# Attention with rotary embedding, then an MLP: batch 0's queries rotated in two parts, tables loaded by ScalarE, squares summed by adds

## The chip, the core and the metric

The kernel runs on one core of a Trainium2 chip. The core has five engines that run side by side, each with its own queue in order: TensorE (PE; matrix products, with weight loads as PEld), VectorE (DVE), ScalarE (ACT), GpSimd (POOL) and SyncE (SP), which here issues DMA transfers. The metric is the device time of one execution in microseconds; lower is better.

## The reference

Attention over 4 batches of 8 heads, 576 positions of 64 columns, then an MLP over the 2304 rows of 512 that come out:

```python
q_rot, k_rot = rotate(q), rotate(k)          # x1*cos - x2*sin, x1*sin + x2*cos
scores = (q_rot @ k_rot.T) / 8
attn = exp(scores - max); attn = attn / (sum(attn) + 1e-9)
x = (attn @ v), heads side by side           # 2304 x 512
h = x @ w_in                                 # 512 x 2048
g = s * relu(h)**2 + b
out = g @ w_out                              # 2048 x 512
```

`w_in` and `w_out` arrive as float64 words and are turned into float32 on the chip.

## The kernel before

**Tiling.** Two heads make a pair, so there are 16 pairs, four to a batch. The 576 positions of a pair are 4 x 128 main rows and a tail of 64 for each head; a score tile is 128 queries by 576 keys, nine tiles to a pair (i = 0 to 8, the ninth holds both tails). The 2304 rows of x are cut into nine units: unit 0 and units 1 to 7 of 256 columns each (two to a batch), and unit 8 with the tails of all batches.

**Two precisions.** Batch 0 (pairs 0 to 3, `FQ`) works in float32: key and query are rotated (`rotate`, three VectorE or GpSimd steps: x times sine into z, x times cosine in place, x plus z), transposed on TensorE (`qk_T`) and copied out of PSUM (`qk_ev`); `s_pair` makes the scores of two tiles at once. The later pairs are split into a high and a low float16 half and transposed by DMA. Then, for every tile: `s_max` (VectorE, the row maximum), `s_exp` (ScalarE), the sum's reciprocal, and the scaled tile as float16 in two halves (`p_a`, `p_b`, the tile pab), which SP transposes by DMA into pt. For two tiles (i = 0 and 2) of each pair of batch 0 TensorE transposes instead. `pv_sum` multiplies pt by v, and `o_out` (ScalarE) writes the result into x.

**The weights.** 32 blocks of 512 KB are loaded, made into float32 (`w_sign`, `w_low`, `w_rebias`, `w_join`), measured (`w_gram` on TensorE, `w_max` on VectorE), and once all 16 of a matrix are there, split into float16 halves (`w_hi`, `w_lo`).

**The MLP.** Unit 0 runs in float32 early on (`mlp_in0`, `mlp_out0`). The other eight units need a power-of-two scale for x: `x_norm` (ScalarE) squares x into bfloat16, `x_sum` (TensorE, L828) sums the squares over the 512 columns of d by four products with a matrix of ones, one for each slot of 128, `x_scale` (VectorE, seven short steps, the first a maximum) makes the scale, `x_hi` and `x_lo` the float16 halves. Then 16 blocks of `mlp_in` (L863), the squared relu, its halves g, and `mlp_out` (L930).

**What sets the order.** `plan()` lists the work as pieces with the engines that may do each and the tokens that it reads and writes. ORDER is a permutation of these pieces, two characters for each; PICKS says which engine does a piece that several could do; SLOTS says which buffer of a kind a piece takes. The pieces are issued in that order, so each engine's queue is a part of it, and an engine whose next instruction waits does nothing else meanwhile. SP's queue holds all DMA issues. PSUM has two banks px for short results.

**The start.** SP issues the rope table (cosine, sine, minus sine, 432 KB), the identity, the first key, the first v, a weight block and the first two queries.

Of the kernel before, what the change touches and what calls it, by code (L numbers as in the profile page):

```python
# [20 lines left out]
GP = 4  # L21
P_SCALE = 2.0 ** 14
# [16 lines left out]
    "AADTEBADDUEAD_AJDcDdECEDEEDeDfEFDiDgELDhEMAEEIENAFAMDjALA3AKANAdDkDlJjAGA5EJAHAfA6AeDrDpAgDsJkAhEGA4JlA9DqEHEKA7DtJrJsJt"  # L39
    "DyA-DVAOAIEODuAPDvDwD1DxJuJmDWDXD2D3EPESEQBAAwAWDYJnDZAXA_DzBBJoEXEVAYJvAZD6AxAzD7ERAyD0A0AaEeAqArDaEYEZEfD4EWD5AtEaEhEb"  # L40
    "DbAQJ0BCJpA8D8ATEsAjAmASAsEcAuEgARJ8ETJ1AlAkJ9J2J-DmBRBEJ3JqAUJ_AnBDEiEdBTBFBUEjEvE5ErBGABD9BrEkAiBSAoAvBHA1A2BIE6KAJ4Bt"
    "BVEmElEnBxJwEoJxDnKFAVAbB0ByKNApKGBsBXEuJ5BzE2B1BYD-DoKHKOBZBaKIKJBbBuEpBKKPJ6J7BMFGBeFFFJBvK4BgKQBLK5AcBNBOE7JyK6KKBfLA"
    "KBBJBPJzKCLBB2BwBQK7FILCBhBkBWKLKWBcFTE3BiFULDB3BlEtBnBmEwKMKRB4KeKXKDLEB7B6CSLFKfKYBoB5E4KSKnFhB-BdK8FVKZKEB8KaKgKTFQCU"
    "CVKhKvKbKUClKiK9CTKcCWBjBpB_CBKoKwKdCABqCCKpCoKqKxKjK-B9CDLJCEKrLKCmEqKkCnCpLLKlCLCNKsKyLRcdLrCYACKmLMLNKVKzCOCbLSLTKtLs"
    "CMLULOLVbMbNbObLK_LGLtCabPLHLIbQLuCZCPCyFHCsC1C0EULWLPK0CcLacebRLiExEycfLvEzLjLkF7cgCtE0E1CuFKE-F-CzC2chLlLbbSbTCvCXCdCe"
    "ciLmE_CwMRMSLnLXLQLYE8C_CFDBLcDCLdLeLwLZMTMUDADDLfCHLgbWbXbYbVbZbaFkK1KuL3MVL4MECfDMF6bgK2bfL5MFE9LxFRCIChCiF9K3L0MCbiL1"
    "MWcjbhbjDNCgL2CGbUbkCJbbCxC3MXGHGICjMDDPL6MGFSL7ckC4LhLoLpLqL_MdCQCKb2b0L8DOMHMeMAFAMIC5DGFfLyMBLzCRMqC6MfMLL9L-MMMJCkCq"
    "M3bcb3M4CrMNMrMKFiC8M5C7M6clFLb1DHFMcmC9FNFOFPM7Fqb4b5M8MabdDEC-MbMoMcFYM9MgDQMhMpMlMsFWcncoMtMONANBNOFCMiMxMmDFFDMZFrDI"
    "MuMvFXMjMybeb6b7blDRb8cpMQNPNCDJMPDKNDNQNENRNFNGNSMnF5MwMkMYMzFEFZNHNTcqbmbnbsNmDLbpbqbrN0DSNnNIF8NXNUNJNLNoFgbtbucrGVFa"
    "FBM0FsGENVGFNYFcN1FjM1M2NdGGNeNMNfNgNhNicBFlcAb_Npb-NqFmN2FnNjNrNscCcDN3M_M-NKFdNZNNNWFtFuFvdDNtFoFecsboODbvdEbwb9cEN4Fp"  # L50
    "dFOEFwFyNxNuctN5GJFxNydGOFcuN9dHFzdINaOROGcFcJcGN6NccvF2NbN-OHcwOINvOSN7F_GAcIOUcLcKOJHJcxOKcyGTFbOVGBOTNzGUGYGXczOLGCGD"
    "OMNlF3NwN8N_NkOkOWc0OlcMOOOPcNOXOYcHcUOhbxcOOiGWc1c2OcOZOdGhF4GiOmOjc3F0OAOyOzOaOCOBc4dwO0GMc5OeGvF1ONOvcScPdxbycQOwGKdy"
    "dzc6d0OxOnOoO1d1d2c7bzO2d3d4OpGNGLd5cTcVP7O_cRd6eFeGcWO6HMc8GuOQObGQGRGtc9cXGjGec-P8c_eHOsdAdBOqOtdCO7GfeIO3d7d8P9d9cYcZ"
    "d-dJdKeJd_O4eAdLPCOfOgeQcaGZcbPDdMdNGxGyPAP-ePGaPBccPEdOdPGwPFPQeBPNeDeCG7GbGcGgeKGddQPGPRPOP_GOGPO8OrO5OueRPHPKeSPSPIG4"
    "PLGSPPejPTQAPUdReLekelPdeZeEPgdSPYQBG8dTdUGkemGmPVeTeMO9eaeUdVGlPePfPZPhPiO-ebPjeceddWPWeOeNPueVdXdYGzPreXe4PvPsPkenPtPJ"
    "PMPaHHPXdZG9daPlPwPxeoPyPodbG0G1dceee3efQHddQIG2P2e5e6PzeWeYQEehPbepdeerQFPpPmdfdgP3QGQJQKQLG3dhQSQTQUP0diQVegeteiQWQPHK"
    "euQvPcQXQYdjfCQseqesPnPqP4P1GnHSQZHTQQe7QdQedkQwevewQtexQxGoHIeydldmdnP5QMQaP6QuQyHAdoQzQbHBe8Qje0eze1fBfOfPe2Q3fDfEfQQk"
    "QlfRQNG5G6e-dpQ9Q6fAQmfSfTfUHLdqQRGpHjQDQcQfQCQOdre9e_fFfGQnQ-Q7Q0QoQ_Q4fVQ1fWQ8G-RAQpG_RBfXHiRFdsHlfIRXfHRzQgR0R1QifYHC"
    "dudtdvRYRCHUfZfaR2RDQhHvRGQ2Q5H7QrQqfbfcRZRURVHwfdfkHVRWRaRERHfJfjRlHNRiHOHPHQR3HRfKftfuHeRjRbfLfMHYfeR4HZHWRfRgRcRdR5fl"
    "ffRkfhfmfnfofgfiRLRIRmHXRMHaH-fvRnfwRoHbRpRqIGfqR8fpf4R9fxRtRKfsRNRrHxfyR_SARJgLf3gMROGqR-SBHhHkSCSeRuRPIHSNfrfzf0f2H8HD"  # L60
    "RhfNGrRvReSDRQRRSfH_gNRsf5IJRTRSIISOHsSgSEf6f7f8SKSFSLSHgOSPSIf1gBgPgQSMSQSRgCgDSbRwgEHmgFSVGsgGScSSSdHnf9Spf-f_gHShSWHo"
    "RxRyHcHfH9SsgJgRgWgVgASGSJR7HpHqSTSiHrStSUR6SXSqHtSuSjSkHuIKHyHESrSvTHgIS5gfgKgXHzSwSxH0gYS0gZIAILgaSYgSgUgcH1H4SZSagsTI"
# [69 lines left out]
def plan():  # L132
# [32 lines left out]
    def prep(pr):  # L165
# [12 lines left out]
        for nm in "kq":  # L178
            add((DVE, POOL), "rotate", pr, nm, steps=3, r=[("tab",)], w=[(nm, pr), ("z", pr, nm)])
# [144 lines left out]
def tile_rope_attention__then__relu2_mlp(  # L324
# [13 lines left out]
    nc = tc.nc  # L338
# [716 lines left out]
```

## Time and profile before

| | us |
|---|---|
| median of 3 runs (lowest, highest) | 620.26 (618.44, 623.89) |
| the profiled execution | 619.45 |
| its span, first to last instruction | 617.5 |
| TensorE busy in the span | 585.6 (95%) |
| VectorE, ScalarE, GpSimd busy | 468.6, 409.8, 123.7 |
| mean granted TensorE clock | 0.996 of 2.4 GHz |

Rows of the profile begin with the time from the span's start and a duration, both in us; what stands behind them is the engine, the source line, the operation and the tiles that it writes and reads (out<-in), and xN counts instructions. A square bracket tells how long the engine stood idle before and what released it. A busy share is an average over stages with different limits, so the stages are read one by one. Durations of instructions on one engine overlap a little where they follow one another.

### The profile page before, as it was taken

How to read it: one execution, taken by the hardware profiler on the slowest of the kernel's cores; microseconds unless marked ns; L12 is line 12 of the kernel's file. 1: busy time of each engine (PE TensorE's matmuls, PEld its weight loads, DVE VectorE, ACT ScalarE, POOL GpSimd, SP SyncE). 2: the span in 40 equal slices, each digit the busy share in tenths (PEclk: the TensorE clock that was granted, in tenths of full speed). 3: DMA queues.
4: the chain of work that ended last, by engine and by line, in shares of the span. 5: the costliest groups of instructions: out<-in, count | busy, mean ns of one | idle time of the engine just before them, and what ended most of it. 6: DMA issues, size and time to landing. Idle time of an engine off the chain costs nothing.

```text
span 617.5 us, 12373 instructions
## 1 busy us (share of the span) xinstructions
PE 585.6 (95%) x4634; PEld 394.9 (64%) x4634; DVE 468.6 (76%) x1023; ACT 409.8 (66%) x860; POOL 123.7 (20%) x131
## 2 busy tenths in 40 slices
PE   3689989899999999999999999999999999999996
PEld 2466767575766656666766676657666766766763
DVE  6999889699999999988978998888883536623111
ACT  3589888777989787877656685747672444542341
POOL 1132323232111221441111103122110101100100
PEclk9999999899999999999999999999999999999999
DMA  8887899598874699787895885686670040650100
GB/s 307 296 256 250 236 243 240 92 208 200 176 175 90 120 192 186 158 198 141 169 193 83 159 189 120 110 164 141 135 152 22 34 78 2 134 131 1 35 1 34
DMA packets 209867, 90.32 MB, mean 146 GB/s; under 512 B 192272, under 2 KB 196496, under 8 KB 209808
## 3 DMA queue, kind: packets, MB, share of 16 engines
q1 hardware_dynamic: 209808, 89.54, 64.8%
q8 instruction: 36, 0.59, 0.4%
q14 instruction: 23, 0.19, 0.1%
HBM read 31.97 MB, written 4.72 MB: 59 GB/s over the span
## 4 chain that ended last, share of the span: by engine, by line
PE 72%; DVE 10%; DMA 9%; ACT 4%; issue 3%; POOL 1%; SPq 0%; DVEq 0%; ACTq 0%; POOLq 0%
PE px L863 25%; PE po L930 23%; PE px L741 8%; PE s L656 7%; PE px L889 4%; DMA pt<-pab 3%; DMA st_k<-in_k_dram 3%; PE po L906 3%; DVE s L662 2%; DMA x<-in_moe_w_in_dram 2%; DMA x<-in_moe_w_out_dram 2%; ACT p L391 1%; PE s L638 1%; DVE pab L388 1%; DVE wio L388 1%
## 5 line engine op out<-in xcount | busy, mean ns | idle before, releaser
L930 PE MATMUL po<-wio,g 128*128 128x512 f16 x768 | 185.0, 379 | 0.0
L863 PE MATMUL px<-xa,wio 128*128 128x256 f16 x1536 | 181.0, 273 | 0.0
L863 PEld LDWEIGHTS <-wio 128*128 128x128 f16 x1536 | 148.5, 98 | 32.6 <-issue 2.7
L391 ACT ACTIVATE p<-s,nm 128x576 f32<-128x576 f32 x144 | 105.8, 736 | 75.8 <-DVE s L662 58.5
L388 DVE SCALAR_TENSOR_TENSOR pab<-p,sum,pab 128x576 f16<-128x576 f32 x136 | 115.1, 858 | 12.9 <-ACT pab L391 7.3
L930 PEld LDWEIGHTS <-g 128*128 128x128 f16 x768 | 70.3, 98 | 73.7 <-issue 3.0
L662 DVE TENSOR_SCALAR_CACHE_REDUCE s<-s,sc 128x576 f32<-128x576 f32 x108 | 87.6, 820 | 14.0 <-PE s L657 13.2
L391 ACT ACTIVATE hr<-px,xc 128x512 f32<-128x512 f32 x64 | 43.6, 682 | 62.6 <-PE px L863 62.4
L881 POOL TENSOR_TENSOR g<-hr,g 128x512 f16<-128x512 f32 x34 | 41.7, 1225 | 203.9 <-ACT g L391 92.1
L391 ACT ACTIVATE pab<-p,sum 128x576 f16<-128x576 f32 x77 | 58.0, 765 | 6.9 <-DVE sum L690 4.8
L741 PE MATMUL px<-pt,v 128*64 128x320 f16 (+2 forms) x640 | 52.6, 286 | 5.2 <-DMA pt<-pab 5.2
L385 POOL TENSOR_SCALAR pab<-p,sum 128x576 f16<-128x576 f32 x31 | 27.1, 875 | 119.0 <-DVE sum L690 88.3
L741 PEld LDWEIGHTS <-v 128*64 128x64 f16 x640 | 35.9, 111 | 17.1 <-issue 11.5
L391 ACT ACTIVATE hr<-hr 128x512 f32<-128x512 f32 x68 | 42.6, 627 | 1.4
L656 PE MATMUL s<-qkT 128*128 128x512 f16 (+1 forms) x120 | 41.4, 384 | 0.6 <-ACT p L391 0.6
L656 PE MATMUL s<-kS,qkT 128*128 128x512 f16 (+1 forms) x120 | 41.3, 380 | 0.0
L765 DVE CAST g<-hr 128x512 f16<-128x512 f32 x25 | 10.6, 425 | 37.8 <-ACT hr L391 37.5
L656 PEld LDWEIGHTS <-qkT 128*128 128x128 f16 (+1 forms) x240 | 22.0, 100 | 24.3 <-issue 5.0
L881 DVE TENSOR_TENSOR g<-hr,g 128x512 f16<-128x512 f32 x30 | 20.5, 687 | 17.6 <-ACT g L391 17.3
L662 DVE TENSOR_SCALAR_CACHE_REDUCE s<-s 128x576 f32<-128x576 f32 x36 | 27.0, 766 | 8.9 <-PE s L638 8.9
L889 PEld LDWEIGHTS px<-x,wio 128*128 128x128 f32 x256 | 30.4, 192 | 3.8 <-issue 2.6
L889 PE MATMUL px<-x,wio 128*128 128x128 f32 x256 | 32.8, 280 | 0.0
(143 smaller groups left out, 836.4 us busy)
## 6 DMA issues: line engine op xcount, KB each, us to landing
x<-in_moe_w_in_dram SPq DMA_DIRECT2D x16, 512.0 KB, 4.9
x<-in_moe_w_out_dram SPq DMA_DIRECT2D x16, 512.0 KB, 4.4
st_v<-in_v_dram SPq DMA_DIRECT2D x16, 320.0 KB, 3.8
st_k<-in_k_dram SPq DMA_DIRECT2D x16, 288.0 KB, 3.6
st_q<-in_q_dram SPq DMA_DIRECT2D x16, 288.0 KB, 3.4
out_dram<-o SPq DMA_DIRECT2D x7, 512.0 KB, 4.2
kS<-qkT SPq DMA_DIRECT2D x24, 144.0 KB, 2.8
pt<-pab SPq DMA_TRANSPOSE x152, 3.0
```

The source lines that it names most:

```text
L385: eng.tensor_scalar(out=out, in0=in0, scalar1=s1, scalar2=s2, op0=op0, op1=op1)
L388: nc.vector.scalar_tensor_tensor(out=out, in0=in0, scalar=scalar, in1=in1, op0=op0, op1=op1)
L391: nc.scalar.activation(out=out, in_=in_, func=func, **kw)
L656: nc.tensor.matmul(ps[rows, MAIN:2 * MAIN], lhs, kk[:, h:8:2], start=(n == 0), stop=(n == 1))
L662: nc.vector.tensor_scalar(out=T["s"], in0=T["s"], scalar1=-1.0 / 8.0 if pr in FQ else st[pr]["es"], scalar2=None, op0=ALU.mult, op1=ALU.mi ...
L741: nc.tensor.matmul(o[64 * h:64 * h + 64, c], v_rows(pr, h, k, z), p_rows(pr, 2 * (i // 4) + h)[:, k, c], start=((z, k) == todo[0]), stop=( ...
L765: nc.vector.tensor_copy(out, in_)
L863: nc.tensor.matmul(ph, w16[0][:, f, wz, cc], X["xa"][:, xz, c], start=(c == 0 and n == 0), stop=(c == NC - 1 and n == 2))
L881: (nc.vector if eng == DVE else nc.gpsimd).tensor_tensor(out=g[:, 1], in0=r, in1=g[:, 0], op=ALU.subtract)
L889: nc.tensor.matmul(ph, wi[:, f + 1, c * P:(c + 1) * P], xs[0]["x"][:, c, j * P:(j + 1) * P], start=(c == 0), stop=(c == NC - 1))
L906: nc.tensor.matmul(X["po"][:, j * DM:(j + 1) * DM], gs["h", j, f - f % 4][:, f % 4 * P:(f % 4 + 1) * P], wo[:, f + 1], start=(n == 1), sto ...
L930: nc.tensor.matmul(po, g[:, gz, jj], w16[1][:, f, wz], start=(n == 1 and i == 0), stop=(n == NF and i == 2))
```

## The change

Five edits, and a new table of order, picks and slots:

- The rope table becomes two tiles, sine with minus sine (288 KB) and cosine (144 KB). ScalarE issues their loads and the identity's ahead of its first instruction; SP issues none of them.
- In batch 0 the rotation of a query is two pieces: `rotate_a` turns columns of the first two of nine slots, 128 of 576, `rotate_b` the other 448. The first part is transposed into a px bank by itself (`q_Ta`) and copied by `q_eva`; `qk_T` and `qk_ev` do the rest. The first `s_pair` of a pair needs only the first part of the query and the key.
- `x_add` is new: two adds in place on VectorE or GpSimd fold the squares' four slots into two and into one. `x_sum` is one product of ones instead of four.
- `warm` is new: twelve pieces of eight products of ones with ones (128 columns, bfloat16) into a px bank, whose result nobody reads.
- ORDER, PICKS and SLOTS are written anew.

```diff
+WARM = 12
...
-        for nm in "kq":
-            add((DVE, POOL), "rotate", pr, nm, steps=3, r=[("tab",)], w=[(nm, pr), ("z", pr, nm)])
+        for nm in "k" if F else "kq":
+            add((DVE, POOL), "rotate", pr, nm, steps=3, r=[("sin",)], w=[(nm, pr), ("z", pr, nm)])
         if F:
...
+            add((DVE, POOL), "rotate_a", pr, steps=3, r=[("sin",)], p=[("q", pr)], w=[("qa", pr), ("z", pr, "a")])
+            add((DVE, POOL), "rotate_b", pr, steps=3, r=[("sin",)], p=[("q", pr)], w=[("qb", pr), ("z", pr, "b")])
+            add(PE, "q_Ta", pr, r=[("qa", pr), ("eye",)], p=[("q", pr)], w=[("bank", "Ta", pr)])
+            add((ACT, DVE), "q_eva", pr, r=[("bank", "Ta", pr)], p=[("qkT", pr)], w=[("fa", pr)])
...
-            add(PE, "s_pair", *c, r=[("qkT", pr)], w=[("s", c), ("s", (pr, i + 2))])
+            add(PE, "s_pair", *c, r=[("qkT", pr)] if i else [("fa", pr), ("fk", pr)], p=[] if i else [("qkT", pr)], w=[("s", c), ("s", (pr, i + 2))])
...
         add(ACT, "x_norm", u, r=[xk], w=[("g", ("n", u))])
+        add((DVE, POOL), "x_add", u, steps=2, w=[("g", ("n", u))])
...
-    def load_tab():
-        nc.sync.dma_start(out=tab, in_=rope)
-        nc.sync.dma_start(out=ident, in_=eye)
+    def load_sin():
+        nc.scalar.dma_start(out=tsin.rearrange("p t h e -> p (t h e)"), in_=rope[:, 0:576])
+
+    def load_cos():
+        nc.scalar.dma_start(out=tcos.rearrange("p t e -> p (t e)"), in_=rope[:, 576:864])
+
+    def load_eye():
+        nc.scalar.dma_start(out=ident, in_=eye)
...
+    def warm(n):
+        o = bank()[:, 0:P]
+        for i in range(8):
+            nc.tensor.matmul(o, ones16b, ones16b, start=True, stop=True)
...
+    def rotate_a(pr, e):
+        yield from turn(st[pr]["q"], slice(0, 2), e)
+
+    def rotate_b(pr, e):
+        yield from turn(st[pr]["q"], slice(2, 9), e)
...
+    def x_add(u, e):
+        eng, x = nc.vector if e == DVE else nc.gpsimd, xs[u]["xq"]
+        for n in (2, 1):
+            eng.tensor_tensor(out=x[:, 0:n], in0=x[:, 0:n], in1=x[:, n:2 * n], op=ALU.add)
+            yield
...
     def x_sum(u):
         X = xs[u]
         X["xn"] = bank()[:, 0:UN]
-        for c in range(NC):
-            nc.tensor.matmul(X["xn"], ones16b, X["xq"][:, c], start=(c == 0), stop=(c == NC - 1))
+        nc.tensor.matmul(X["xn"], ones16b, X["xq"][:, 0], start=True, stop=True)
```

Of the tables the first line shows the kind of difference:

```diff
 ORDER = (
-    "AADTEBADDUEAD_AJDcDdECEDEEDeDfEFDiDgELDhEMAEEIENAFAMDjALA3AKANAdDkDlJjAGA5EJAHAfA6AeDrDpAgDsJkAhEGA4JlA9DqEHEKA7DtJrJsJt"
...
+    "DiAADhABDwDxDyDtDuDvACADDzAIAEDqDrAXEYDsEjD3AaAYAZEkBFEXAREZAbD1ElD-D9EpArBIBGD0EgEmD8DjD4D2KFBHEhANEaBJKNEnEiEqAUD_EAEB"
```

**VectorE from its first rotation on.** z is the product with the sine, st_k and st_q are the loaded key and query. Before:

```order
L573 TENSOR_TENSOR z_124<-st_k_110,tab 128x9x2x32
L575 TENSOR_TENSOR st_k_110<-st_k_110,tab 128x576
L545 TENSOR_REDUCE mx<-px_127 128x1
L577 TENSOR_TENSOR st_k_110<-st_k_110,z_124 128x576
L573 TENSOR_TENSOR z_137<-st_q_116,tab 128x9x2x32
L383 TENSOR_SCALAR sc<-px_127 128x1
L575 TENSOR_TENSOR st_q_116<-st_q_116,tab 128x576
L573 TENSOR_TENSOR z_149<-st_q_118,tab 128x9x2x32
L577 TENSOR_TENSOR st_q_116<-st_q_116,z_137 128x576
```

And in the changed kernel, where GpSimd's first three instructions are the steps on the first query's other 128 columns:

```order
L598 TENSOR_TENSOR z_115<-st_q_109,tsin 128x7x2x32
L600 TENSOR_TENSOR st_q_109<-st_q_109,tcos 128x448
L602 TENSOR_TENSOR st_q_109<-st_q_109,z_115 128x448
L598 TENSOR_TENSOR z_153<-st_k_112,tsin 128x9x2x32
L600 TENSOR_TENSOR st_k_112<-st_k_112,tcos 128x576
L602 TENSOR_TENSOR st_k_112<-st_k_112,z_153 128x576
L598 TENSOR_TENSOR z_161<-st_q_158,tsin 128x2x2x32
L397 TENSOR_SCALAR wio<-x_156 128x512 x2
L600 TENSOR_TENSOR st_q_158<-st_q_158,tcos 128x128
```

The query goes first and is 448 columns wide here; the key follows, and no short step of v's scale stands between them. Up to the sixteenth `w_max` VectorE's queue holds 13 whole rotations before, and 8 whole ones, four of 448 columns and one of 128 now; two more of the integer casts of a weight block and two more casts into pab, and one score maximum fewer.

**TensorE from the first transposes to the first scores.** s is a score tile or a transposed operand, px a bank. Before:

```order
L748 MATMUL s_141<-ident,st_k_110 128x128 x4
L751 MATMUL s_141<-ident,st_k_110 64x64 x2
L748 MATMUL s_168<-ident,st_q_116 128x128 x4
L751 MATMUL s_168<-ident,st_q_116 64x64 x2
L638 MATMUL s_176<-qkT_159 128x512
L638 MATMUL s_177<-qkT_159 128x512
L638 MATMUL s_176<-qkT_159 128x64
L638 MATMUL s_177<-qkT_159 128x64
```

Now:

```order
L782 MATMUL s_163<-ident,st_q_109 128x128 x3
L785 MATMUL s_163<-ident,st_q_109 64x64 x2
L782 MATMUL s_182<-ident,st_k_112 128x128 x4
L785 MATMUL s_182<-ident,st_k_112 64x64 x2
L801 MATMUL px_194<-ident,st_q_158 128x128
L672 MATMUL s_212<-qkT_200 128x512
L672 MATMUL s_213<-qkT_200 128x512
L672 MATMUL s_212<-qkT_200 128x64
L672 MATMUL s_213<-qkT_200 128x64
L564 LDWEIGHTS ones16b
```

Three blocks of products of ones stand ahead of these rows and a fourth behind them; before, the first v's gram stood ahead and the second's behind.

**VectorE at the scale of one unit.** g holds the squares, xm their maximum, xs the scale. Before:

```order
L388 SCALAR_TENSOR_TENSOR pab_3707<-p_3656,sum_3655,pab_3707 128x576
L383 TENSOR_SCALAR pab_3771<-p_3457,sum_3456 128x576
L388 SCALAR_TENSOR_TENSOR pab_3703<-p_3667,sum_3655,pab_3703 128x576
L835 TENSOR_REDUCE xm<-px_3774 128x1
L385 TENSOR_SCALAR xs_3779<-xw,xm 128x2
L383 TENSOR_SCALAR xs<-xs_3779 128x2
```

Now:

```order
L696 TENSOR_SCALAR s_3814,nm_3880<-s_3814,sc 128x576
L872 TENSOR_TENSOR g_3887<-g_3887 128x512
L872 TENSOR_TENSOR g_3887<-g_3887 128x256
L402 SCALAR_TENSOR_TENSOR pab_3871<-p_3795,sum_3794,pab_3871 128x576
L885 TENSOR_REDUCE xm<-px_3925 128x1
L399 TENSOR_SCALAR xs_3938<-xw,xm 128x2
```

The two adds stand behind a score maximum and ahead of a pab pass; seven units have them on VectorE, the last one on GpSimd. On TensorE 24 `mlp_in` and 9 `mlp_out` products stand between the last unit's closing pv products and its product of ones, where 12 and 9 stood.

## Rows read from the trace of the kernel before

**Rows 1.** Stages: us, busy us of PE, PEld, DVE, ACT, POOL; granted clock, DMA share, GB/s.
```profile
0.00:40.00 40.00, 22.78 (x144) 16.11 (x144) 33.40 (x75) 22.56 (x43) 7.88 (x13) 1.00 0.84 290
40.00:80.00 40.00, 36.45 (x341) 26.90 (x340) 37.64 (x90) 37.74 (x88) 12.47 (x17) 1.00 0.87 250
80.00:110.00 30.00, 28.28 (x272) 20.92 (x270) 26.32 (x67) 26.25 (x61) 8.38 (x11) 1.00 1.04 226
110.00:150.00 40.00, 36.84 (x247) 23.88 (x246) 32.65 (x77) 29.07 (x64) 13.16 (x11) 0.96 0.76 168
150.00:600.00 450.00, 448.88 (x3571) 300.52 (x3570) 335.79 (x715) 290.25 (x602) 80.67 (x79) 1.00 0.60 122
```

**Rows 2.** What TensorE waited for in the span: us in total, times, longest us.
```profile
PE px L741 <- DMA pt<-pab: 5.2, 6, 1.9
```

**Rows 3.** The first 18 us in order of time: start us, us, engine, line, operation.
```profile
0.73 1.28 ACT L391 ACT_TABLE_LOAD   x1 [0.73 <-PEq L1032]
...
0.74 0.40 SPq L514 DMA_DIRECT2D tab<-in_rope_dram  x1
...
1.66 0.43 SPq L511 DMA_DIRECT2D st_k<-in_k_dram  x1
...
5.53 0.76 DVE L573 TENSOR_TENSOR z<-st_k,tab 128x576 f32<-128x576 f32 x1 [4.36 <-DMA st_k<-in_k_dram]
...
13.78 2.40 PE L638 MATMUL s<-qkT 64*128 64x512 f32 x8 [0.75 <-ACT qkT L391]
...
16.64 0.77 DVE L662 TENSOR_SCALAR_CACHE_REDUCE s<-s 128x576 f32<-128x576 f32 x1
```

**Rows 4.** The chain that ended last: start us, us, what.
```profile
1.66 3.78 DMA st_k<-in_k_dram
...
114.04 3.74 PE px L741 x27
...
132.10 2.15 PE px L741 x28
...
171.94 5.31 PE px L863 x48
...
541.43 5.83 PE po L930 x27
```

**Rows 5.** VectorE by form: instructions | busy us, mean ns | idle before, releasers.
```profile
L383 DVE TENSOR_SCALAR pab<-p,sum 128x576 f16<-128x576 f32 x28 | 14.7, 529 | 0.5 <-issue 0.2
...
L383 DVE TENSOR_SCALAR wio<-x 128x512 uint16<-128x512 uint16 x19 | 10.1, 530 | 0.3 <-DMA x<-in_moe_w_out_dram 0.3
```

**Rows 6.** Timeline, passes of GpSimd and VectorE that overlap or stand alone.
```profile
11.32 0.67 POOL L385 TENSOR_SCALAR x<-x 128x512 f32<-128x512 f32 x1 [2.65 <-DMA x<-in_moe_w_in_dram]
...
11.36 1.23 DVE L575 TENSOR_TENSOR st_q<-st_q,tab 128x576 f32<-128x576 f32 x1
...
27.41 1.01 POOL L385 TENSOR_SCALAR x<-x 128x512 f32<-128x512 f32 x1 [2.06 <-ACT qkT L391]
```

**Rows 7.** Timeline before and at the last sum of squares.
```profile
559.18 0.47 ACT L391 ACTIVATE x<-px,sc 128x256 f32<-128x256 f32 x1 [3.56 <-PE px L741]
...
559.69 1.06 ACT L391 ACTIVATE g<-x 128x1024 bf16<-128x1024 f32 x1
...
562.33 0.60 PE L828 MATMUL px<-g,ones16b 128*128 128x256 bf16 x4
```

**Rows 8.** The page, part 5, the subtractions of 512 columns.
```profile
L881 POOL TENSOR_TENSOR g<-hr,g 128x512 f16<-128x512 f32 x34 | 41.7, 1225 | 203.9 <-ACT g L391 92.1
...
L881 DVE TENSOR_TENSOR g<-hr,g 128x512 f16<-128x512 f32 x30 | 20.5, 687 | 17.6 <-ACT g L391 17.3
```

**Rows 9.** Stages around the wait at 112 us, columns as in Rows 1.
```profile
114.00:116.00 2.00, 1.96 (x16) 1.75 (x17) 0.17 (x1) 0.31 (x2) 2.00 (x3) 0.53 0.00 0
```

**Rows 10.** TensorE in order of time, four key transposes early and later.
```profile
28.00 1.08 PE L748 MATMUL s<-ident,st_k 128*128 128x128 f32 x4 [1.05 <-ACT qkT L391]
...
36.37 0.60 PE L748 MATMUL s<-ident,st_k 128*128 128x128 f32 x4
```

More of the change, by code (lines that the diff above doesn't have):

```diff
@@ L138, in add @@
             for i in range(steps):
-                add(engs, fn, *a, r=r, w=w, p=p)
+                add(engs, fn, *a, r=[*r, ("cos",)] if i == 1 and ("sin",) in r else r, w=w, p=p)
                 work[-1]["step"] = i
@@ L215, in attend @@
                 t = j % 2
-                add((ACT, DVE, POOL), "p_diag", *c, r=[("r", (pr, g)), ("tab",)], w=[("dg", c)])
+                add((ACT, DVE, POOL), "p_diag", *c, r=[("r", (pr, g)), ("eye",)], w=[("dg", c)])
                 add(PE, "p_T", *c, r=[("p", c), ("dg", c)], w=[("po", c)])
@@ L300, in unit @@
             add(DMA, "store", u, js, r=[("o", u, j) for j in js] + [("ot", u)])
-    add(DMA, "load_tab", w=[("tab",)])
+    add(DMA, "load_sin", w=[("sin",)])
+    add(DMA, "load_cos", w=[("cos",)])
+    add(DMA, "load_eye", w=[("eye",)])
+    for n in range(WARM):
+        add(PE, "warm", n, w=[("bank", "warm", n)])
     for i in range(2):
@@ L565, in scales, with turn @@
             stt(d["es"], d["iv"][:, 0:1], -1.0 / 8.0, d["iv"][:, 1:2], ALU.mult, ALU.mult)
-    def rotate(pr, nm, e):
+    def turn(x, t, e):
         eng = nc.vector if e == DVE else nc.gpsimd
-        x = st[pr][nm].rearrange("p t (h e) -> p t h e", h=2)
-        cos = tab[:, :, None, 0:32].to_broadcast([P, 9, 2, 32])
-        sin = tab[:, :, 32:96].rearrange("p t (h e) -> p t h e", h=2)
-        z = new(rp, "z", [P, 9, 2, 32], F32)
+        x = x[:, t].rearrange("p t (h e) -> p t h e", h=2)
+        n = t.stop - t.start
+        cos = tcos[:, t, None].to_broadcast([P, n, 2, 32])
+        sin = tsin[:, t]
+        z = new(rp, "z", [P, 9, 2, 32], F32)[:, t]
         eng.tensor_tensor(out=z[:, :, ::-1], in0=x, in1=sin, op=ALU.mult)
@@ L746, in qk_T @@
         x, o = d[nm], new(ps_s, "s", [P, 1024], F32)
-        for t in range(4):
+        for t in range(nm == "q", 4):
             nc.tensor.transpose(o[:, t * P:(t + 1) * P], x[:, 2 * t:2 * t + 2].rearrange("p h d -> p (h d)"), ident)
@@ L752, in qk_T, with both @@
         d["T", nm] = o
-    def qk_ev(pr, nm, eng):
+    def both(pr):
         d = st[pr]
@@ L757, in qk_ev, with q_Ta, q_eva @@
             d["F"] = new(stk, "qkT", [P, 2, 9, P], F16).rearrange("p i u m -> p i (u m)").bitcast(F32)
-        f = d[nm + "F"] = d["F"][:, "qk".index(nm)]
-        copy(eng, f, d.pop(("T", nm))[:, 0:576])
+            d["qF"], d["kF"] = d["F"][:, 0], d["F"][:, 1]
+        return d["F"]
+    def qk_ev(pr, nm, eng):
+        i, c = "qk".index(nm), slice(P if nm == "q" else 0, S)
+        copy(eng, both(pr)[:, i, c], st[pr].pop(("T", nm))[:, c])
+    def q_Ta(pr):
+        o = st[pr]["Ta"] = bank()[:, 0:P]
+        nc.tensor.transpose(o, st[pr]["q"][:, 0:2].rearrange("p h d -> p (h d)"), ident)
+    def q_eva(pr, eng):
+        copy(eng, both(pr)[:, 0, 0:P], st[pr]["Ta"])
     def copy(eng, out, in_):
@@ L995, in _rope_table @@
     rows[:, 8] = 512 + np.arange(p) % 64
-    table = np.concatenate([cos, sin, -sin], axis=-1)
-    return np.ascontiguousarray(table[rows].astype(np.float32))
+    parts = [t[rows].reshape(p, -1) for t in (np.concatenate([sin, -sin], axis=-1), cos)]
+    return np.ascontiguousarray(np.concatenate(parts, axis=-1).astype(np.float32))
 def _rows_of(x, name):
```

130 lines of the change are left out of this document (68 added, 62 removed).

## The prediction, made before the changed kernel ran

> **What bounds the kernel now.** I read the stages first, then what TensorE waits for, then the chain of waits, then the rows of the places that the change touches. By stage [rows 1], TensorE is busy 22.78 of the first 40 us, 36.45 of the next 40, 28.28 of the 30 after that, 36.84 of 40 up to 150, and 448.88 of 450 up to 600. So there are two kernels in one. From 150 us on TensorE is the bound and only work taken off it counts. Before that it stands idle for 17.2 + 3.6 + 1.7 + 3.2 = 25.7 us, and something else feeds it: from 40 to 80 us VectorE is busy 37.64 and ScalarE 37.74 of 40, so both are full there and TensorE is not. The list of what TensorE waits for names one releaser often, the transposed tiles pt, 5.2 us in six waits [rows 2]; the rest of its idle time is spread thin.
>
> The start is a chain of its own [rows 3]. SP issues the rope table at 0.74 and the first keys only at 1.66; these take 3.78 us in the chain [rows 4], and VectorE turns the first key from 5.53. The first score products start at 13.78 and the first row maximum at 16.64.
>
> **The change, part by part.** The sum is made against the profiled execution's 619.45 us (span 617.5); the median of the three runs shown is 620.26, 0.8 us higher, and these runs lie 0.9% apart, so about 1% is what a measurement here can tell from no change.
>
> *Tables begun by ScalarE.* Two issues, the table's and the identity's, leave SP's queue, so its first load (now a query) goes out at 0.74 instead of 1.66. If it takes the same 3.78 us, VectorE starts at about 4.6: **0.9 us earlier**, bounds 0 (the sine table, issued at the same moment by ScalarE, lands last) and 0.9. The table is cut in two, and the first step needs only 288 of its 432 KB, so I take 0.9. ScalarE pays three issues of about 0.4 us (SP's table issue took 0.40 [rows 3]) ahead of its function-table load of 1.28 us, which began at 0.73: done by 3.2 us, before any data has landed. The cover is its idle start; nothing else is queued there.
>
> *Query in two parts.* VectorE's share of the first query falls from 576 to 448 columns, at 0.76 us for 576 [rows 3] some 0.59 us for each of three steps, and GpSimd turns the other 128 columns beside it. VectorE thus has 1.8 + 2.3 us in front of the first key's transposes and ends at 4.6 + 4.1 = 8.7. Before, the scores started 13.78 − 5.53 = 8.25 us after the first step; now about 6.4 us after it, at some 11.0, and the first maximum at some 13.5 to 14. That alone is worth little at the end, since VectorE is full from its first step on; what counts is how much work it has. Count its queue up to the sixteenth weight maximum, the last of the weights: before, 13 whole rotations (13 × 3 × 0.76 = 29.6 us); now 8 whole ones, four of 448 columns and one of 128 (18.2 + 7.1 + 0.5 = 25.8). That is 3.8 us less. Against it stand two more integer casts of 0.53 and two more pab casts of 0.53 [rows 5], one score maximum fewer (0.77, [rows 3]) and some single-column operations: about 1.9 us back. **VectorE has 1.9 us less to do** there. Bounds: 0, if ScalarE, as full as VectorE in that stretch and given four more small copies, holds the pace; 1.9, if VectorE does. The two are level in 40 to 80 us, so I take half, **1.0**.
>
> GpSimd works beside VectorE for this. In the rows, a rotation step of VectorE took 1.23 us where it ran beside GpSimd's 0.67 us pass at 11.32, and 0.76 otherwise; but at 27.41 it was GpSimd that took 1.01 [rows 6]. So one step of the first query may lose 0.47 us, from which I take nothing, as it can fall on either engine. The Trainium skill (GPSIMD Engine Reference, § 1. Specifications) says that GpSimd shares its SBUF interface with VectorE and that they contend when a VectorE instruction reads two SBUF inputs, which a rotation step does. By that rule all three steps of the first query stretch, 1.4 us, and the sum below would come to 616.4 instead of 615.0; the rows show it for some overlaps only.
>
> *Squares summed by adds.* TensorE ran four products with ones for each of eight units [rows 7]; now one. In a steady stretch 48 products of the same 256 columns take 5.31 us, 0.11 each [rows 4], so 8 × 3 × 0.11 = **2.6 us** leave an engine that is busy 448.88 of 450 us [rows 1]. The adds come in: 512 and then 256 columns in place, seven pairs on VectorE, the last on GpSimd. Nearest rows [rows 8]: 0.69 us for a 512-column subtraction on VectorE, 1.23 on GpSimd. With half for the second add, a pair costs at most 1.0 on VectorE and 1.8 on GpSimd; at least 0 beyond what their queues have free. VectorE is busy 335.79 of 450 in that stage, so 7 us more is hidden in total; the latency is the risk (below). For the last unit: after the closing pv products, TensorE has 24 products of 256 columns and 9 of 512 before the product of ones (24 × 0.11 + 9 × 0.216 = 4.6 us, the second from 27 in 5.83 [rows 4]); ahead of that product stand the copy of 0.47, the squares of 1.06 [rows 7] and GpSimd's 1.8, in all 3.4. Covered by 1.2 us.
>
> *Products of ones.* 96 products of 128 columns in twelve blocks of eight. At no more than 0.11 each a block takes 0.9 us, all twelve 10.6, against 20.8 us of TensorE's idle time in the first 80 us. Taken at 0; what lies behind a block in the queue (a transpose, a gram) can be late by up to 0.9 us where the block starts late.
>
> *The order.* I find no further term in it: the last unit ends in a run of `mlp_out` as before, so the tail is the same.
>
> Sum: 619.45 − 0.9 − 1.0 − 2.6 = **615.0 us**.
>
> **Rivals.**
>
> 1. *The stall at 111 to 118 us goes too.* There TensorE waited 1.9 us for a transposed pt, the longest of the six [rows 2], and 27 products after it took 3.74 us where 28 took 2.15 later [rows 4]; the granted clock in 114 to 116 is 0.53, so for most of it the 1.2 GHz level [rows 9], against 1.00 in the stages up to 110 us [rows 1]. An order searched anew shifts this wait; if nothing takes its place the kernel gains another 1.9 + 1.6 = 3.5: 611.5. For it: a wait of that size is single in the profile. Against: the pt tiles still pass SP's one queue.
>
> 2. *The products of ones raise the clock early.* Four transposes took 1.08 us at 28.00 and 0.60 at 36.37 [rows 10]: the lower rate holds for the first 36 us, though the granted clock reads 1.00 there, with TensorE busy 22.78 of 40. If the fill-in work brings the higher rate from the first scores on, two transpose groups save 0.48 each and the first block of 2.40 us [rows 3] half of itself, 2.2 us in all, of which VectorE's full queue lets about half through: 613.9. The Trainium skill (TensorE: Matmul & The Clock Gate, Part 1) says that the default is the throttled state and activity releases it; that speaks for this case.
>
> 3. *The relief does not arrive.* ScalarE or the weight loads hold the first 110 us, a new wait for pt eats the rest, and only the squares count: about 617, or 619.5 if a stall of 2 to 3 us is new.
>
> 4. *Slower: the adds become a wait.* TensorE works in order, so where it reaches the one product of ones before the adds are done, everything behind stands still. The adds lie in VectorE's queue behind score maxima and pab passes, and the units in the middle have less in front of the product than the last one. If the adds were wholly uncovered, 7 × 1.0 + 1.8 = 8.8 us, giving 615.0 + 8.8 = 623.8, slower than before. It decides where TensorE's work between the pv products and the product of ones is shorter than copy, squares, adds and whatever stands between them on VectorE. Against it: the last unit has 1.2 us to spare.
>
> **The numbers.** Forecast 0.46, with a range of its own of 613.7 to 617 (start or relief missing at the top, all of both at the bottom). Rival 1: 0.17; rival 2: 0.13; rival 3: 0.16; rival 4: 0.08. The range that should hold 8 of 10 goes from 610.5 (rivals 1 and 2 together, with a little of the bounds) to 619.5 (rival 3 with its stall). 1% below the median is 614.1, 1% above 626.5. Faster by over 1%: rival 1, two thirds of rival 2 and the lower edge of the forecast, 0.35. Slower by over 1% needs rival 4 with waits on top: 0.05. Within 1%: 0.60.
>
> **What would show it.** VectorE's first rotation step near 4.6 us and the first scores near 11; GpSimd's three steps beside it, and whether VectorE's are over 0.6. TensorE's idle time up to 150 us: about 23 to 24 instead of 25.7. Eight products of ones over the squares, with no TensorE wait for VectorE or GpSimd at them; such waits of about 1 us each would mean rival 4. The granted clock from 100 to 150 us: 1.00 throughout means rival 1. Transposes of four near 0.6 us before 30 us mean rival 2. The forecast is wrong if the first scores come near 11 us and the stretch from 80 to 150 us still ends where it did, for then VectorE was not what held it.

## The result: 0.7% slower, and the profile after

The changed kernel took 623.01 us (median of 20 runs, 621.31 to 627.54), the kernel before, beside it, 619.04 us (20 runs, 616.29 to 623.89). The ratio is 1.0071, with a 95% interval of 1.0053 to 1.0088: slower by 4.4 us by the ratio, where 615.0 had been forecast, within 610.5 to 619.5. The profiled execution took 622.75 us, its span 621.0. Ratios leave out slow executions; the profile of changed_again (below) fell on one, 760.98 us at a mean granted clock of 0.753, and nothing is read from it.

The stages of the kernel after, columns as in [rows 1]:

```profile
0.00:40.00 40.00, 24.71 (x212) 18.49 (x212) 32.77 (x76) 22.94 (x45) 11.95 (x20) 0.87 0.84 288
40.00:80.00 40.00, 37.70 (x369) 28.11 (x371) 38.24 (x98) 39.55 (x93) 14.54 (x17) 1.00 0.86 257
80.00:110.00 30.00, 29.07 (x268) 20.82 (x265) 26.93 (x68) 23.16 (x55) 7.89 (x9) 1.00 1.06 224
110.00:150.00 40.00, 35.28 (x244) 22.52 (x241) 32.56 (x76) 27.73 (x62) 14.46 (x13) 0.96 0.79 157
150.00:600.00 450.00, 445.70 (x3538) 297.03 (x3539) 329.47 (x706) 293.21 (x605) 110.63 (x100) 1.00 0.60 122
```

TensorE's idle time up to 150 us fell from 25.7 us to 23.2, inside the forecast's "23 to 24". But the busy time that replaced it is products of ones, and the stage from 150 to 600 us, which was full (1.1 us idle), now has 4.3 us idle. Behind 600 us TensorE is busy 15.21 us of 21.0, before 12.40 of 17.5: 0.7 us more idle. So of the 3.5 us that the span grew, 3.2 + 0.7 are late idle time and −2.6 the squares; the remaining 2.2 us are, by this sum, work that the first 150 us left undone.

What TensorE waited for, after:

```profile
PE px L775 <- DMA pt<-pab: 6.3, 7, 2.6
PE px L801 <- POOL st_q L602: 5.9, 1, 5.9
PE px L564 <- DVE wmx L476: 3.2, 2, 2.3
```

The line that answers to [rows 2] grew from 5.2 to 6.3, and two releasers are new: GpSimd's part of the first query (it stands in the place of a first wait of 6.3 us for the first v before), and VectorE, for which a block of products of ones waits (it needs a px bank).

The start, after, in order of time (rows of several engines):

```profile
0.73 0.40 ACTq L528 DMA_DIRECT2D tsin<-in_rope_dram  x1
...
5.32 0.62 DVE L598 TENSOR_TENSOR z<-st_q,tsin 128x448 f32<-128x448 f32 x1 [4.15 <-DMA tsin<-in_rope_dram]
5.37 0.89 POOL L598 TENSOR_TENSOR z<-st_q,tsin 128x128 f32<-128x128 f32 x1 [4.93 <-DMA tsin<-in_rope_dram]
6.34 0.62 DVE L600 TENSOR_TENSOR st_q<-st_q,tcos 128x448 f32<-128x448 f32 x1 [0.39 <-DMA tcos<-in_rope_dram]
6.38 0.90 POOL L600 TENSOR_TENSOR st_q<-st_q,tcos 128x128 f32<-128x128 f32 x1
7.00 0.76 DVE L602 TENSOR_TENSOR st_q<-st_q,z 128x448 f32<-128x448 f32 x1
7.36 0.72 POOL L602 TENSOR_TENSOR st_q<-st_q,z 128x128 f32<-128x128 f32 x1
...
8.11 0.76 DVE L598 TENSOR_TENSOR z<-st_k,tsin 128x576 f32<-128x576 f32 x1 [0.35 <-POOL st_q L602]
...
8.40 2.13 PE L564 MATMUL px<-ones16b 128*128 128x128 bf16 x16
...
10.32 0.84 PE L782 MATMUL s<-ident,st_q 128*128 128x128 f32 x3
...
11.51 1.11 PE L782 MATMUL s<-ident,st_k 128*128 128x128 f32 x4
...
13.67 1.30 PE L672 MATMUL s<-qkT 64*128 64x512 f32 x8 [0.35 <-ACT qkT L405]
```

Against [rows 3]: the first rotation starts at 5.32 instead of 5.53, not at 4.6, because it now waits for the sine table, and the first scores at 13.67 instead of 13.78, not at 11. They run in 1.30 us instead of 2.40, so TensorE was at its upper rate there. It did not stay there; the stretch from 20 to 30 us, columns as above:

```profile
20.00:30.00 10.00, 7.49 (x55) 5.74 (x54) 9.89 (x25) 6.64 (x14) 2.51 (x4) 0.51 0.76 248
```

The chain that ended last, after, where it answers to [rows 4]:

```profile
110.88 4.31 DMA pt<-pab
115.23 3.66 PE px L775 x27
```

The stall at 112 to 118 us is still there. TensorE waited 2.65 us for pt (1.9 before [rows 2]), and the 27 products behind it took 3.66 us (3.74 before [rows 4]).

### The profile page after: what moved, and what is told of

It reads as the page before. It is cut to its first block, busy times and chain, and to the rows that moved or that the text cites. A ratio compares the mean times of both kernels' runs of the same rounds, so it can differ in the third digit from the quotient of the medians.

```text
span 621.0 us, 12544 instructions
## 1 busy us (share of the span) xinstructions
PE 587.7 (95%) x4706; PEld 394.8 (64%) x4706; DVE 462.9 (75%) x1026; ACT 409.5 (66%) x859; POOL 161.8 (26%) x161
## 4 chain that ended last, share of the span: by engine, by line
PE 69%; DVE 10%; DMA 8%; ACT 7%; issue 3%; POOL 2%; SPq 1%; DVEq 0%; POOLq 0%; ACTq 0%
PE px L913 23%; PE po L980 21%; PE px L775 8%; PE s L690 6%; DMA pt<-pab 4%; PE px L939 2%; DVE s L696 2%; PE po L956 2%; DMA x<-in_moe_w_out_dram 2%; ACT p L405 2%; DVE wio L402 2%; DVE pab L402 1%; PE s L672 1%; POOL wio L399 1%; ACT pab L405 1%
## 5 line engine op out<-in xcount | busy, mean ns | idle before, releaser
L402 DVE SCALAR_TENSOR_TENSOR pab<-p,sum,pab 128x576 f16<-128x576 f32 x136 | 118.3, 881 | 7.3 <-POOL pab L399 4.6
L405 ACT ACTIVATE pab<-p,sum 128x576 f16<-128x576 f32 x73 | 55.2, 769 | 15.0 <-DVE sum L724 7.7
L399 POOL TENSOR_SCALAR pab<-p,sum 128x576 f16<-128x576 f32 x34 | 29.7, 875 | 81.1 <-DVE sum L724 34.1
L405 ACT ACTIVATE g<-hr 128x512 f16<-128x512 f32 x41 | 25.3, 624 | 10.0 <-PE po L980 9.5
```

The costliest lines, as they stand in the source:

```text
L399: eng.tensor_scalar(out=out, in0=in0, scalar1=s1, scalar2=s2, op0=op0, op1=op1)
L402: nc.vector.scalar_tensor_tensor(out=out, in0=in0, scalar=scalar, in1=in1, op0=op0, op1=op1)
L405: nc.scalar.activation(out=out, in_=in_, func=func, **kw)
```

## The experiments

Each ratio is against the kernel before, run on the same chip beside it; the chips differ between groups of runs. The main theory was that the new order loses what the adds save; the rivals were the products of ones, the adds as a wait, and an early loss.

**Products of ones left out.** In `warm`, the eight products and the bank that they write are dropped.

```diff
-        o = bank()[:, 0:P]
-        for i in range(8):
-            nc.tensor.matmul(o, ones16b, ones16b, start=True, stop=True)
+        pass
```

> The changed kernel without its 96 products of ones; order, buffers and everything else as they are. In the changed kernel's trace the twelve blocks take some 9.6 us of TensorE in the first 70 us and the first scores still come at 13.67 us. Theory A (the new order costs the time, the blocks only fill idle time): within 0.5 us of the changed kernel, 622.5 to 623.5. Rival B (the blocks hold up what stands behind them in TensorE's queue): 1.5 to 3 us faster than the changed kernel, 620 to 621.5. Rival C (they raise the clock and so help): 1 us or more slower than the changed kernel, with transposes of four at 1.1 us for longer.

Measured: 620.21 us, ratio 1.0033 (1.0010 to 1.0056). The blocks cost 2 to 3 us, the size that rival B had named, and the theory that they only fill idle time fell. Whether rival B's reason holds is tested further down. Without the blocks the first scores start earlier and run at the lower rate:

```profile
13.16 2.40 PE L670 MATMUL s<-qkT 64*128 64x512 f32 x8
```

**Squares by four products again** (in the changed kernel, adds dropped):

```diff
-            eng.tensor_tensor(out=x[:, 0:n], in0=x[:, 0:n], in1=x[:, n:2 * n], op=ALU.add)
...
+        for c in range(NC):
+            nc.tensor.matmul(X["xn"], ones16b, X["xq"][:, c], start=(c == 0), stop=(c == NC - 1))
```

> The changed kernel with the squares summed by four products of ones again and no adds; order as it is. If each product of ones costs TensorE 0.11 us in a stage where it is the bound, 24 more cost 2.6 us: 625.6. If the adds are a wait that eats the saving (the rival on which the forecast put 0.08), no change or a gain: 622 to 623.

Measured: 626.88 us, ratio 1.0132 (1.0099 to 1.0164), against 1.0069 to 1.0120 for the changed kernel on three chips. By these ratios the adds gain between 0.7 and 3.9 us in the new order. They are hardly a wait there; TensorE waits for them once in the changed kernel:

```profile
PE px L878 <- DVE g L872: 0.3, 1, 0.3
```

**The adds in the old order.** The kernel before with `x_add` put in at hand-chosen places and one product of ones per unit.

> The kernel before, its order, picks and buffers kept, with the two adds put in (GpSimd for the last, tail unit, VectorE for the seven others) and one product of ones for each unit; the product moved by one or two pieces where it stood right behind the squares. Theory A (squares gain 2.6 us by themselves and the searched order is what loses): about 2.6 us less than the kernel before, ratio 0.996. Rival (the adds become a wait): ratio 1.000 or above.

Measured: 624.15 us, ratio 1.0089 (1.0058 to 1.0119). Here the fourth rival happened. Of its waits (engine, line waited for; us in total, times, longest):

```profile
PE px L869 <- DVE xa L389: 3.3, 4, 1.4
...
PE px L834 <- DVE g L828: 1.8, 2, 1.0
```

L834 is the product of ones, L869 the first `mlp_in` behind it. Together 5.1 us, twice the 2.6 saved. VectorE's adds stand in a queue that was laid out without them. Other places for them were not tried.

**Two halves of two orders.** First the new order up to 155 us with the old one behind it, then the reverse.

> The changed kernel's first 830 pieces in its own order (until about 155 us), all later pieces in the order and with the picks of the kernel before, with the same adds as in before_adds. Theory A (the loss is mostly waits of TensorE after 150 us and in the tail, 3.2 + 0.7 us more idle time than before): about 3 to 4 us less than the changed kernel, near 619. Rival (the loss sits in the first 150 us, where 2.2 us less useful work got done): within 1 us of the changed kernel, 622 to 624.

Measured: 629.05 us, ratio 1.0166 (1.0136 to 1.0196).

> The kernel before in its own order for its first 800 pieces (until about 155 us; tables loaded by SyncE, whole queries rotated, no products of ones), all later pieces in the order and with the picks of the changed kernel, squares summed by adds. Theory A (with its 3 us more of waits after 150 us the new late order loses what the adds save): 0 to 1 us from the kernel before, ratio 0.999 to 1.002. Rival (the early part is what loses): 2 us or more below the kernel before, ratio 0.996 or less. Should the seam itself cost, as in the opposite graft, a wait near 155 to 175 us will show it.

Measured: 620.71 us, ratio 1.0048 (1.0023 to 1.0072). The first has 9.0 us of idle time on TensorE between 150 and 600 us, of which 2.18 and 1.42 are two single waits at 165 and 177, just behind the seam, so it says little on the order. The second has 3.7 us of idle time there, like the changed kernel, and loses 3 us although it has the adds. That points to the late part of the new order; what the seam costs is not separated, and its profile (span 617.0 us, no longer than before's 617.5) does not show where the 3 us go.

**The order alone.** The changed kernel without products of ones, with four products per unit and with the tables loaded by SyncE:

```diff
-        nc.scalar.dma_start(out=tsin.rearrange("p t h e -> p (t h e)"), in_=rope[:, 0:576])
+        nc.sync.dma_start(out=tsin.rearrange("p t h e -> p (t h e)"), in_=rope[:, 0:576])
```

> The changed kernel with three of its edits undone: no products of ones, squares by four products and no adds, tables and identity loaded by SyncE at their places in the order. What is left of the change is the new order and the first query's rotation in two parts. Theory A (the new order loses 3 to 4 us by waits after 150 us and in the tail, where the forecast set nothing): 3 to 6 us above the kernel before, ratio 1.005 to 1.010. Rival (the order costs nothing and the loss is in the edits): 0.997 to 1.002.

Measured: 622.79 us, ratio 1.0068 (1.0043 to 1.0093): the order, with the query in two parts, costs 4.2 us. Its stage from 150 to 600 us, columns as above:

```profile
150.00:600.00 450.00, 445.26 (x3546) 298.31 (x3545) 324.90 (x690) 289.79 (x597) 107.37 (x98) 1.00 0.58 121
```

4.7 us are idle, with no adds in the kernel. On the same chip, with adds and ScalarE's loads but no products of ones:

> The changed kernel without products of ones, once more, beside the changed kernel on the same chip. Theory A: 2 to 3 us less than the changed kernel, 1.001 to 1.004 of the kernel before. Rival: within 1 us of the changed kernel.

Measured: 620.89 us, ratio 1.0042 (1.0020 to 1.0064). So squares and tables together bring 1.9 us, with an interval of about 1.5 us on either of the two times.

**Waits taken out of the order by hand.** Ten pieces of TensorE moved (the expectation counts twelve), so that products that are ready stand ahead of eight waits (4.5 us in that trace).

> The changed kernel without products of ones, and twelve pieces of TensorE moved by a few places, so that products that are ready stand ahead of a piece that TensorE waited at without products of ones (pt 0.88 us at 145, 0.26 at 159, 0.90 at 283, 0.25 at 315, 0.54 at 406, 0.25 at 466; the adds 0.41 at 289; score slots 1.02 at 340). Nothing is added or left out beside the products of ones. Theory A (these waits are what the new order loses, since TensorE is the bound there): 2 to 4 us less than without products of ones, 616.5 to 618. Rival (the waits move to the next piece, or the bound after 150 us is elsewhere): within 1 us of it, 619.5 to 620.5.

Measured: 619.90 us, ratio 1.0024 (0.9999 to 1.0048), within the interval of the kernel it was made from. The rival held. Its stage:

```profile
150.00:600.00 450.00, 445.60 (x3538) 295.49 (x3538) 331.09 (x707) 292.32 (x603) 110.77 (x101) 1.00 0.59 122
```

The idle time is 4.4 us, 4.2 without the repair: the eight waits went, and new ones of 0.26 to 0.73 us came at nine other places (for score slots, pt, xa, g, the adds). So the waits came back at other pieces.

**The relief of VectorE, undone.** Without products of ones, the first parts of three queries' rotations moved from GpSimd to VectorE (three letters of PICKS).

> The changed kernel without products of ones and with the first parts of three queries' rotations moved from GpSimd to VectorE (128 columns, about 0.28 us for each of nine steps, 2.5 us in all). The forecast's step (VectorE's work in the first 70 us sets the pace, half of what is taken off it arrives): 1 to 1.3 us slower than without products of ones. Theory A (ScalarE and the weight loads hold that stretch; GpSimd's 0.9 us steps hold the first transposes): equal or up to 0.5 us faster, with the first transpose near 7.8 us instead of 7.9 to 8.1.

Measured: 621.56 us, ratio 1.0047 (1.0027 to 1.0067), on the chip where 1.0042 was measured without this edit. The first transposes came at 8.31 us, the first scores at 14.08 instead of 13.33, and the first product of unit 1 at 170.10 instead of 171.22. Neither the later start nor 2.5 us more work on VectorE shows at the end by more than the interval, about 1.3 us.

**Which products of ones.** First three blocks kept, then the complement (`if n not in (0, 5, 1): return` and its opposite):

> The changed kernel with three of the twelve blocks of products of ones, those that stand around and ahead of the first query's transposes; the other nine blocks are taken out. Without any, 620.2 against 623.0 us was measured. Theory A (the price is paid at the start: 16 products ran at 8.40 to 10.53 us ahead of the first query's transposes, which began at 10.32 instead of 8.19): most of the price stays, 622 to 623. Rival B (the price is spread over all blocks, or lies in the later nine): 620 to 621.

Measured: 619.58 us, ratio 1.0010 (0.9983 to 1.0037).

> The complement: the three blocks at the start are taken out, the nine later ones stay. Theory A (price at the start): 620 to 621, as without any. Rival B: 622 or more. If both kernels stand near 621.5, every block costs about 0.25 us.

Measured: 618.60 us, ratio 1.0013 (0.9989 to 1.0037). Neither part has the price, so neither theory was right. Both also stand below the kernels without any (1.0033 and 1.0042), but those ran on other chips. The chip could have made the difference, so the changed kernel was taken again on two more chips.

> The changed kernel itself, once more, as the base for the three beside it. Earlier 1.0071 of the kernel before; with none of the products of ones 1.0033, with three blocks 1.0010, with nine 1.0013. Theory A (the products of ones cost about 2.5 us, and only all twelve together): 1.006 or above. Rival (chance and the chip made most of that difference): 1.002 to 1.005.

Measured: 626.77 us, ratio 1.0120 (1.0085 to 1.0156), beside the 1.0042 without any.

> The changed kernel once more, as the base on the same chip for the three beside it. So far 1.0071 and 1.012 of the kernel before; without products of ones 1.0033 and 1.0042, with only three or nine of the twelve blocks 1.0010 and 1.0013, but on other chips. Theory A (all twelve blocks together cost 2 to 5 us): 1.006 to 1.012. Rival (the chip made the difference): 1.003 or less.

Measured: 623.19 us, ratio 1.0069 (1.0046 to 1.0093). On this chip stood also nine blocks, ten blocks (`if n in (5, 1): return`), and twelve blocks of one product each (`range(1)`):

> Nine blocks as in later_nine_ones, once more on the same chip as the changed kernel. Theory A: 1.000 to 1.004, at least 2 us less than the changed kernel. Rival (the chip made the difference): within 1 us of the changed kernel.

Measured: 618.77 us, ratio 0.9984 (0.9955 to 1.0012).

> The changed kernel without the two blocks that ran at 8.40 to 10.53 us, between the first part's transpose and the rest of the first query's; the first block and the nine later ones stay. Theory A1 (those two blocks hold back the first scores, and that delay is the price): 1.001 to 1.004. Rival (no one block is to blame): near the changed kernel, 1.006 or above.

Measured: 619.25 us, ratio 1.0001 (0.9978 to 1.0023).

> The changed kernel with all twelve blocks in place, each of one product of ones instead of eight: the blocks' waits for a px bank stay, their time on TensorE goes. Theory A1 (TensorE's time in the blocks ahead of transposes is the price): as without any, 1.002 to 1.005. Theory A2 (a block's wait for its bank, 2.35 us behind VectorE's weight maximum at 26.20, holds the queue and is the price): as the changed kernel, 1.006 to 1.012.

Measured: 619.84 us, ratio 1.0009 (0.9979 to 1.0039). So the chip is not the cause: all twelve cost 3.4 to 4.4 us against any of the three. Against none at all they cost 5.9 us by the medians on the chip before (626.77 and 620.89). The wait for a bank is not the price either, since one product per block keeps it.

One transfer sets the four profiles of kernels with twelve full blocks apart. The pt that ends the stall takes 4.31 us in the changed kernel (above), and in the same kernel on another chip:

```profile
112.05 4.81 DMA pt<-pab
116.90 2.09 PE px L775 x27
```

With nine blocks:

```profile
109.43 2.92 DMA pt<-pab
112.39 2.09 PE px L777 x27
```

It took 4.31 to 4.81 us in all four profiles with twelve, and 2.91 to 2.96 in all ten others of this early order up to here. The DMA view of 111 to 112 us in the changed kernel shows what lies inside it (queue, kind; packets, MB, share):

```profile
q8 instruction: 1, 0.02, 5.5%
```

That is a load of instructions. In the ten others none lies inside this transfer. By the same view, between two bursts of this transfer's packets the DMA engines moved 10 GB/s or less for 1.6 us; in ten_blocks, with no load inside, for 0.2 us. In the changed kernel queue 8 has such a load every 11 to 22 us over the whole span; there are 36 in kernels with up to 24 products of ones and 37 in those with 72 or more. The more of these products stand in front, the earlier its loads come: at 107 to 109 us without any, at 97 to 100 and again at 111 to 115 us with nine to twelve blocks. So they are taken for TensorE's. Two last kernels separate the instructions from their time.

```diff
-        for i in range(8):
+        for i in range(8 if n else 44):
```

> The changed kernel with 44 instead of 8 products of ones in the block that starts at 1.23 us; TensorE waits there until 8.13 us anyway, and 36 more products at 0.13 us end near 7. All four profiles of kernels with twelve full blocks show one instruction load (16 KB, a queue of its own) inside the last transposed pt before the stall at 115 us, and that transfer took 4.31 to 4.81 us; in all others of this order it took 2.91 to 2.93 and the load lay elsewhere. 36 more products move TensorE's instruction loads to an earlier place in its work. Theory I (where the loads fall is the price): the pt transfer takes 2.9 us, the wait at 115 us is under 2.3, and the time is 2 to 4 us less than the changed kernel, ratio 1.000 to 1.004, although 36 products are added. Rival (TensorE's time in the blocks is the price): 1.006 or above.

Measured: 622.99 us, ratio 1.0055 (1.0027 to 1.0083). The load moved to 108 us, and the transfer was short again:

```profile
111.91 2.97 DMA pt<-pab
114.92 2.09 PE px L775 x27
```

The wait before it fell to 1.75 us, as expected, but the time did not fall to 1.004: in this trace TensorE waited 2.00 us for another pt, at 469 us, a transfer of 3.57 us. No load of queue 8 lies inside it, but one of 8 KB on queue 14, another queue of instruction loads:

```profile
468.99 0.96 PE L775 MATMUL px<-pt,v 128*64 128x320 f16 x10 [2.00 <-DMA pt<-pab]
```

Half of theory I's expectation failed, and the interval of the ratio reaches into what either theory expected.

```diff
-        o = bank()[:, 0:P]
+        o = bank()[0:32, 0:1]
...
-            nc.tensor.matmul(o, ones16b, ones16b, start=True, stop=True)
+            nc.tensor.matmul(o, ones16b[:, 0:32], ones16b[:, 0:1], start=True, stop=True)
```

> The changed kernel with all twelve blocks of eight products, but each product on 32 rows of ones and one column: the number of TensorE's instructions stays, most of the blocks' 9.6 us on TensorE goes. With one product in each block the ratio was 1.0009, with all of full size 1.0069. Theory I (where TensorE's instruction loads fall is the price): the load lies inside the last pt before the stall again, that takes 4.3 us or more, and the ratio is 1.005 to 1.009. Rival (TensorE's time in the blocks): pt in 2.9 us, ratio 1.000 to 1.003.

Measured: 624.73 us, ratio 1.0105 (1.0063 to 1.0147), with the load at 114.9 us:

```profile
112.86 4.90 DMA pt<-pab
117.80 2.42 PE px L775 x19
```

The two blocks at the start now take 0.78 us instead of 2.13, and the price is all there (against the kernel before; the changed kernel itself did not run on this chip). So the time of the products on TensorE is not what costs; something is that goes with their number, and not in proportion: ten blocks (80 products) cost no more than one product per block. The clock of the start is not the price either: with the tiny products the first scores stay at the lower rate,

```profile
13.16 2.40 PE L672 MATMUL s<-qkT 64*128 64x512 f32 x8
```

and the granted clock up to 150 us is 0.99 there, 0.95 in the changed kernel and 0.94 with one product per block.

## Why the prediction was wrong

The forecast was 619.45 − 0.9 − 1.0 − 2.6. Step by step:

- **Products of ones, "taken at 0": the step that failed most.** They cost 5.9 us against none on one chip, about 2.4 by the ratios of the result and of no_ones, and 3.4 to 4.4 against fewer products. The reasoning looked for what lies behind a block in the queue and found at most 0.9 us, one block; two blocks stand there, and the first query's transposes did come 2.1 us later (10.32 instead of 8.19). But that is not the price, as tiny_products shows. The twelve blocks bring 192 more instructions (a weight load and a product each), these move TensorE's instruction loads, and in all five profiles with this count one lies inside the transfer that TensorE waits for near 115 us: wait 2.57 to 3.24 us, against 0.29 to 2.29 in the others. In changed_third the wait is 1.5 to 2.3 us longer than in the three others of its chip, and its first `mlp_in` product of unit 1 starts 1.9 to 3.9 us behind theirs (172.72 us against 170.81, 168.79 and 170.02 with ten, nine and one-product blocks). So the transfer accounts for about two of the four microseconds. Where the rest is lost is open: from that product to the end changed_third takes 449.0 us, ten and nine blocks 445.6 and 446.5, but one-product blocks 448.6 and longer_first_block 450.3, both with the short transfer, and behind 150 us TensorE waits in changed_third only 0.5 us for pt, against 2.2 us for VectorE.
- **"The order. I find no further term in it": failed.** It costs 4.2 us (2.7 to 5.7 by the interval). The instructions' order was read at the start and at the end of the program; the 3 us more of idle time lie between 150 and 600 us, in waits of 0.2 to 1.0 us, where [rows 1] had shown the stage full, with 1.1 us idle in 450. A stage so full was a result of its order, and a new order was not owed the same. Why the waits come back when single ones are taken out is not shown.
- **Tables begun by ScalarE, −0.9: did not happen.** The lower bound held: the sine table landed last, 4.57 us after its issue at 0.73, where I had taken the key's 3.78 us [rows 4]. Then VectorE waited 0.39 for the cosine table and 0.35 for the buffer of GpSimd's part.
- **The first scores near 11 us: they came at 13.67.** GpSimd's steps took 0.89, 0.90 and 0.72 us beside VectorE's, and 0.45 later alone; VectorE's first two stayed at 0.62, its third took 0.76. I had let the overlap fall on either engine; it fell on GpSimd, which TensorE waits for. The Trainium skill (GPSIMD Engine Reference, § 1. Specifications) says that the two contend where a VectorE instruction has two SBUF inputs; here the trace shows longer steps on GpSimd. The key is the other part: without the blocks its transposes wait for VectorE until 10.30 us, where 8.7 was forecast, and the scores come at 13.16.
- **VectorE's relief, −1.0: not seen.** Undoing 2.5 us of it changed 620.89 to 621.56, less than the interval. The third rival's first half fits: in the changed kernel ScalarE is busy 39.55 of 40 us in 40 to 80 (37.74 before), and VectorE still 38.24. That ScalarE is what held the stretch is argued, not shown.
- **Squares, −2.6: right in mechanism, and in size as far as can be told.** 1.9 us with the tables on one chip. That the adds are covered held in the new order (0.3 us); in the old one they were a wait, 5.1 us.
- **Rivals.** The first did not happen: the stall grew. The second happened in part: four key transposes at 1.11 us are followed by scores in 1.30 us at 13.67, so TensorE's rate rose before 14 us, as the Trainium skill (TensorE: Matmul & The Clock Gate, Part 1) says that activity releases the throttle. By its own sign, transposes of four near 0.6 us before 30 us, it did not, and nothing of it arrived. From 16 to 20 us TensorE was busy 0.83 us, then the granted clock reads 0.51 in 20 to 30 us (its 1.2 GHz level), four transposes took 1.06 us again at 28.63, and the third block of scores starts at 44.00 us with the blocks and at 43.88 and 44.71 in the two profiles of the same kernel without. The fourth was given 0.08 for the adds; what made the kernel slower were two other terms that stood at zero. That its 623.8 lies near the 623.01 measured is chance.

On the one chip where all was run (changed_again, no_ones_again, order_only), the terms add up by the medians: 4.4 us for the order, −1.9 for squares and tables, 5.9 for the products of ones, 8.4 in all.

The range missed the result because both zeros had no upper bound. "Bounds from both sides" was kept for the edits with a row, not for the order and the fill-in work, which had none.

No version here beats the kernel before by more than can be measured. The best, nine blocks of ones, stands at 1.0013 and 0.9984, and 1 lies inside both intervals.

## What to carry to other kernels

A bound engine that is idle only 1 us in 450 owes that to the order: here a new order, and operations put into the old one, started from some microseconds of loss, and mending single waits did not bring them back. Fill-in work on an idle engine isn't free because the engine is idle; ask what its instructions displace, and test it with the same number of tiny ones. Ask of work that starts earlier what the next full engine will let through; here nothing of it was seen at the end.

## What was not expected of the hardware

- A load of 16 KB of TensorE's instructions inside a transposing transfer went with 4.31 to 4.90 us for that transfer, in five profiles of five; without one it took 2.91 to 2.97, in eleven of eleven. Adding 72 instructions moved the load out and the transfer was short again (2.97).
- A 288 KB table issued at 0.73 us beside a key and a query landed at 5.30 us; before, 432 KB from one queue had landed by 5.53, where the first step ran.
- A rotation step of 128 columns on GpSimd took 0.89 us beside VectorE's and 0.45 alone.
